# A delta-rule attention and a maxout network in one kernel: the third group's triangle moves from PSUM to SBUF, and the opening is reordered

## Chip, cores and metric

One NeuronCore of a Trainium2 chip. The metric is device time in microseconds (us), the median of several runs; lower is better.

## What is computed

Two layers. The first is a delta-rule recurrence over 768 positions for 4 batches x 8 heads with head size 48; its output, turned into 3072 rows of 384, goes through a feed-forward layer that takes the maximum of three products.

```python
k_n = k / (np.linalg.norm(k, axis=-1, keepdims=True) + 1e-06)
for t in range(S):
    y[:, :, t] = einsum('bhd,bhde->bhe', q[:, :, t], state)
    v_old = einsum('bhde,bhd->bhe', state, k_n[:, :, t])
    state = state + beta_t * einsum('bhd,bhe->bhde', k_n[:, :, t], v[:, :, t] - v_old)
x = y.transpose(0, 2, 1, 3).reshape(B * S, H * D)
h = maximum(maximum(x @ w1, x @ w2), x @ w3)
out = h @ w_out
```

## The kernel before

**Chunks, units, groups.** The sequence is cut into 12 chunks of 64 positions. A chunk is two *units* (half the batches each), so there are 24 units; two chunks make a *group* (6 in all), and one group gives 512 rows (a *piece*) of the feed-forward layer. Within a chunk the recurrence becomes linear algebra: the products of keys with keys (tile `at`) and of keys with queries (tile `pt`), and a triangular system whose inverse (`ut`) is applied to the values.

**From keys to the inverse.** `turn` transposes keys (part 0) or queries (part 1) of a unit on TensorE (PE) into PSUM and copies them to `kqt`; `gram` (`keys` for part 0 alone) makes the products `p_g` and copies them to `at` or `pt`. `to_blocks` and `first_blocks` bring the first group's 32 x 32 diagonal blocks into `x_bl` by copies and a transpose on VectorE (DVE); later groups go through DRAM (`to_dram`, `blocks`). `solve(m)` inverts a group's blocks by a chain of small DVE operations (L570, L574), one pair for each row. It starts with the norms of the keys (`norm`, from the diagonal of the block). The triangle is built in `y_bl` in SBUF, but for groups 1 and 2 in a PSUM tile `y_p`, which ScalarE (ACT) clears first and from which two copies (L576, L578) bring it back. The first group is solved only in blocks of 16 (`FINE`); `halves_t`, `halves_z`, `halves_u` join these to 32, and `turn_t1`, `join_z`, `join_u` join 32 to 64. Results go back to `ut` with a minus sign, by `negated`.

**Links.** Per chunk: `old_k` (values minus keys times state), `old_q` (queries times state), `new` (`p_u`, the updates `u`), `step` (adds to the state `st`), `to_y` (`p_y`), `to_x` or `y_blocks`/`read_y`/`turn_y` (the output turned into `xt`). The values are multiplied by the norms with `scale` on GpSimd (POOL, L287). For the first two chunks the norms come from squares and row sums of the keys themselves (`first_squares`, `flipped`, `first_norms`).

**Feed-forward.** `ffn(m)` yields after each product `p_h` (L935); the first three column blocks of piece 0 are made in halves of 256 rows (18 products), all others with 512. Then come the output products `p_o` (L967). The result of `p_h` is copied by ACT (L943) or joined by a maximum on DVE (L949).

**Weights.** They lie in 64 bits. `fetch` brings a piece to `w_bits` (5 buffers); each step of the generator `weights` has ACT make three conversions of one piece (L238 to L240, into `mant` and `up`, two buffers each), and then, for the piece before it, a DVE shift (L250) and a POOL addition (L254).

**PSUM.** All results of small products share the tag "two" (three buffers of two banks); `p_h`, `p_o` and `p_m` share the tag "ffn" (two buffers).

**Order.** It is written by hand: each engine executes its instructions in the order in which the program issues them. The opening (L1003 to L1088) is a plain list. Then the loop over `ffn(0)` (L1149) issues after each yield what the tables `FIRST` (links of chunk 1, queries), `EARLY_LINKS` (group 1), `CONVERTED` (steps that convert a weight piece) and `FETCHED` name; later pieces use `LINKS`. A letter in a table is a function (`z` join_z, `j` join_u, `k` old_k, `q` old_q, `u` new, `s` step, `y` to_y, `x` to_x, `e` halves_z, `f` halves_u, `d` turn_t1, `S` steps of the solver, `T` turn, `P` gram), the digit its chunk or unit.

Of the kernel before, what the change touches and what calls it, by code (L numbers as in the profile page):

```python
# [18 lines left out]
BL = 32  # L19
# [4 lines left out]
def kernel(  # L24
# [274 lines left out]

    ksum_0, kflip_0 = small("ksum0", 2, 2, H), small("kflip0", 2, H)  # L300

    def first_squares(units=range(4)):
        ksum, kflip, squares = ksum_0, kflip_0, []
        for n in units:
            c, g = divmod(n, 2)
            if n < 2:
                ksq = work.tile([128, H, D], FP32, name="ksq", tag="o_sb")
            else:
                ksq = in_wo(1).rearrange("p s r -> p (s r)")[
                    :, (n - 2) * H * D : (n - 1) * H * D  # L310
                ].rearrange("p (h d) -> p h d", h=H)
            nc.scalar.square(ksq, kpad[n][:, :, 0:D])
            squares.append(ksq)
        yield
        for n in units:
            c, g = divmod(n, 2)
            ksq = squares[n]
            nc.vector.tensor_reduce(
                out=kflip[:, c] if g else ksum[:, c, 0], in_=ksq,
                axis=mybir.AxisListType.X, op=ALU.add,  # L320
            )

    def flipped(kflip):
        p_n = ps_ffn([128, TOK], "p_n")[:, 0 : 2 * H]
        for bb in range(2):
            half = rows(1 - bb)
            nc.tensor.matmul(
                p_n[rows(bb)], ident[half, half],
                kflip[half].rearrange("p c h -> p (c h)"),
            )  # L330
        return p_n

    def first_norms():
        norm(nrm_0, ksum_0, small("root0", 2, 2, H), small("newton0", 2, 2, H))
# [186 lines left out]
    def solve(m):  # L521
# [8 lines left out]
        if m in (1, 2):  # L530
            y = ps_two("y_p").rearrange("p b (j i) -> p (b j) i", i=BL)
        if m:
            zero = kpad[0][:, 0:1, D : D + 1]
            nc.scalar.copy(y, zero.to_broadcast(y.shape))
        else:
            nc.gpsimd.memset(y_bl, 0.0)
# [4 lines left out]
        nc.vector.reciprocal(bl, bl)  # L541
        nc.vector.tensor_tensor(out=bl, in0=bl, in1=bl, op=ALU.mult)
        nc.vector.tensor_tensor(out=bl, in0=bl, in1=beta_bl[:, m] if m else beta_0, op=ALU.mult)
        if m > 2:
            nc.scalar.copy(diagonal(y), bl)
        else:
            (nc.vector if m else nc.gpsimd).tensor_copy(diagonal(y), bl)
# [10 lines left out]
        for j in range(size - 1):  # L558
# [16 lines left out]
            if m in (1, 2) and j == BL - 8:  # L575
                nc.scalar.copy(done[:, :, 0:HB], y[:, :, 0:HB])  # L576
            elif m in (1, 2) and j == BL - 2:
                nc.vector.tensor_copy(done[:, :, HB:BL], y[:, :, HB:BL])  # L578
            yield
        if m == 0:  # L580
# [3 lines left out]
            for cc in range(2):  # L584
                for i in range(4):
# [6 lines left out]
                    if half:  # L592
                        nc.scalar.copy(to, of)
                    else:
# [75 lines left out]

    def span(hs):
# [16 lines left out]
    def negated(bb, to, of, c=0):  # L688
        if bb and c < 1:
            nc.vector.tensor_scalar_mul(to, of, -1.0)  # L690
        else:
            nc.scalar.mul(to, of, -1.0)

    def halves_u(c):
        t, z = fine.pop(c), zs[c % NU]
        for hs, p_v, _ in heads_of(c, "p_f", BL):
            for i, h in enumerate(hs):
                for bb, g in TILES:
                    r = rows(bb ^ g)
                    nc.tensor.matmul(p_v[rows(bb), g, i], t[g][r, h], z[r, g, h])  # L700
            for f in (0, 1):
                for bb in range(2):
                    r = block(bb, f, HB)
                    negated(
                        bb,
                        ut[c % NU][r, :, span(hs), BL * f + HB : BL * (f + 1)],
                        p_v[r, :, :, HB * f : HB * (f + 1)],
                        c,
                    )

    def join_z(c):
        at = [ats.pop(2 * c + g) for g in range(2)]
        z, second = zs[c % NU], ut[c % NU][:, :, :, BL:C]
        for hs, p_v, _ in heads_of(c, "p_z", BL):
# [6 lines left out]
            nc.scalar.copy(z[block(0), :, span(hs)], p_v[block(0)])  # L721
            copy = nc.vector.tensor_copy if c < 1 else nc.scalar.copy
            copy(z[block(1), :, span(hs)], p_v[block(1)])

    def join_u(c):
        z, t = zs[c % NU], t1[c % NU]
        u12 = ut[c % NU][:, :, :, BL:C]
        for hs, p_v, _ in heads_of(c, "p_j", BL):
            for i, h in enumerate(hs):
                for bb, g in TILES:  # L730
                    r = block(bb ^ g)
                    nc.tensor.matmul(p_v[block(bb), g, i], t[r, g, h], z[r, g, h])  # L732
            for bb in range(2):
                negated(bb, u12[block(bb), :, span(hs)], p_v[block(bb)], c)
# [505 lines left out]
```

## Time and profile before

| | us |
|---|---|
| median of 3 runs | 524.41 |
| those runs | 521.0 to 526.13 |
| profiled execution, own time | 523.37 |
| its span on the core | 521.7 |
| PE busy in the span | 494.0 (95%) |
| DVE busy | 302.0 (58%) |
| POOL busy | 186.2 (36%) |
| ACT busy | 167.0 (32%) |

The profile shows one execution. Times in it count from the start of its span, so the 1.67 us between span and execution lie around it. Its views: the span in 40 slices of 13 us, with the busy tenths of each engine and the clock granted to PE; the busy time of each engine by stage; the timeline of one engine (start, length, operation, and in brackets the idle time before it with what ended it); the list of waits. "PEld" is PE's loading of the stationary operand, "issue" is time in which the engine waited for nothing that the profile shows.

### The profile page before, as it was taken

To read this page: it belongs to the slowest core of one execution; us is meant where nothing else is said; L and a number is where in the kernel's file an instruction comes from. 1 tells how busy PE (TensorE), PEld (TensorE's weight loads), DVE (VectorE), ACT (ScalarE), POOL (GpSimd) and SP (SyncE) were. 2 spreads that over 40 slices of the span, in tenths; PEclk is the share of its full clock that TensorE was granted. 3 is DMA by queue.
4 is the path that set the end of the run, shared out by engine and by line. 5 is a ranking of instruction groups with operands and counts; after the bars stand their busy time and mean duration, and the time that the engine had idled before them with its cause. 6 is when DMAs were issued, how large, how long until landed. Compare 5 with 4: busy or idle time off the path is not lost.

```text
span 521.7 us, 18025 instructions
## 1 busy us (share of the span) xinstructions
PE 494.0 (95%) x7840; PEld 305.5 (59%) x7840; DVE 302.0 (58%) x699; ACT 167.0 (32%) x306; POOL 186.2 (36%) x310
## 2 busy tenths in 40 slices
PE   7667799999899999999999999999999999999996
PEld 6556678845566555665555565655655555654453
DVE  5866998788695441699562988645896221111100
ACT  5557565875413142200143101252101411011000
POOL 6515073772292844851385770503130000000000
PEclk9756999999899999999999999999999999999999
DMA  8973968773035954454585553923334202220011
GB/s 116 215 153 100 172 170 132 184 213 90 3 91 135 183 94 100 104 127 113 116 154 116 127 133 88 171 43 92 81 97 96 41 3 63 61 61 0 0 30 31
DMA packets 108670, 53.45 MB, mean 102 GB/s; under 512 B 91760, under 2 KB 102928, under 8 KB 108592
## 3 DMA queue, kind: packets, MB, share of 16 engines
q1 hardware_dynamic: 97840, 34.44, 32.4%
q0 software_dynamic: 8640, 17.49, 14.0%
q8 instruction: 61, 1.00, 0.9%
q10 hardware_dynamic: 2112, 0.39, 0.5%
q14 instruction: 17, 0.14, 0.1%
HBM read 39.17 MB, written 13.11 MB: 100 GB/s over the span
## 4 chain that ended last, share of the span: by engine, by line
PE 81%; DVE 10%; ACT 3%; POOL 2%; issue 1%; DMA 1%; SPq 0%; DVEq 0%; POOLq 0%; ACTq 0%
PE p_h L935 36%; PE p_o L967 26%; PE p_g L438 4%; PE p_u L777 2%; PE p_m L915 2%; PE p_y L819 2%; PE p_s L800 2%; PE p_q L749 2%; PE p_k L749 2%; PE p_j L732 1%; DVE tmp L570 1%; PE p_z L718 1%; POOL w_sb L254 1%; PE p_t L361 1%; DMA kpad<-in_k_dram 1%
## 5 line engine op out<-in xcount | busy, mean ns | idle before, releaser
L935 PE MATMUL p_h<-xt,w_sb 128*128 128x512 f32 (+1 forms) x522 | 217.7, 561 | 1.7 <-DVE xt L886 1.3
L935 PEld LDWEIGHTS p_h<-xt,w_sb 128*128 128x128 f32 x522 | 95.2, 191 | 86.9 <-issue 80.3
L967 PE MATMUL p_o<-wo_sb,h 128*128 128x384 f32 x288 | 97.8, 489 | 0.0
L949 DVE TENSOR_TENSOR h<-h,p_h 128x512 f32<-128x512 f32 (+1 forms) x48 | 29.6, 617 | 93.9 <-PE p_h L935 93.8
L967 PEld LDWEIGHTS p_o<-wo_sb,h 128*128 128x128 f32 x288 | 53.8, 190 | 35.6 <-issue 0.5
L973 ACT COPY o_sb<-p_o 128x384 f32<-128x384 f32 x24 | 11.5, 479 | 131.3 <-PE p_o L967 128.2
L945 ACT ACTIVATE h<-p_h 128x512 f32<-128x512 f32 x30 | 17.9, 597 | 87.7 <-PE p_h L935 84.7
L967 PE MATMUL p_o<-w_sb,xt 128*128 128x384 f32 x120 | 42.0, 486 | 0.0
L570 DVE TENSOR_TENSOR tmp<-x_bl,y_bl 128x60 f32<-128x60 f32 (+19 forms) x108 | 38.8, 360 | 3.3
L396 POOL DMA_DIRECT2D turned<-in_q_dram x72 | 39.1, 551 | 4.4 <-POOL turned L391 2.6
L574 DVE TENSOR_TENSOR y_bl<-y_bl,tmp 128x60 f32<-128x60 f32 (+19 forms) x108 | 35.7, 330 | 3.7
L438 PE MATMUL p_g<-kqt 48*64 48x64 f32 (+1 forms) x1216 | 28.1, 243 | 7.0 <-DVE nt_bl L263 3.8
L438 PEld LDWEIGHTS p_g<-kqt 48*64 48x64 f32 x1216 | 25.0, 143 | 15.4 <-ACT kqt L367 8.1
L967 PEld LDWEIGHTS p_o<-w_sb,xt 128*128 128x128 f32 x120 | 22.8, 190 | 15.9
L254 POOL TENSOR_TENSOR w_sb<-mant,up 128x384 int32<-128x384 int32 x18 | 18.5, 1027 | 27.4 <-DVE mant L250 26.6
L120 POOL DMA_DIRECT2D kpad<-in_k_dram x32 | 21.8, 689 | 16.4 <-PE p_s L800 14.9
L287 POOL TENSOR_TENSOR v_t<-v_t,nrm 128x768 f32<-128x768 f32 x12 | 17.7, 1482 | 25.7 <-DVE nrm L266 14.2
L807 DVE TENSOR_TENSOR st<-st,p_s 48x768 f32<-48x768 f32 (+1 forms) x18 | 17.1, 950 | 15.3 <-PE p_s L800 15.1
L422 DVE TENSOR_TENSOR pt<-p_g,mask 128x512 f32<-128x512 f32 x20 | 13.8, 690 | 17.4 <-PE p_g L438 17.4
L574 DVE TENSOR_TENSOR y_p<-y_p,tmp 128x31 f32<-128x31 f32 (+15 forms) x62 | 21.6, 349 | 2.1
L139 POOL DMA_DIRECT2D v_t<-in_v_dram x12 | 9.9, 828 | 35.3 <-PE p_u L777 35.3
L391 POOL MEMSET turned<- 128x96 f32 x18 | 3.3, 191 | 46.6 <-DVE kqt L412 46.6
(158 smaller groups left out, 631.8 us busy)
## 6 DMA issues: line engine op xcount, KB each, us to landing
w_bits<-in_moe_w_dram SPq DMA_DIRECT2D x14, 384.0 KB, 5.5
out_dram<-o_sb SPq DMA_DIRECT2D x48, 96.0 KB, 2.2
turned<-in_q_dram POOLq DMA_DIRECT2D x72, 48.0 KB, 2.8
kpad<-in_k_dram POOLq DMA_DIRECT2D x32, 96.0 KB, 5.2
y_x<-y SPq DMA_DIRECT2D x16, 192.0 KB
qall<-y_x SPq DMA_DIRECT2D x32, 96.0 KB, 2.7
ut<-y_d SPq DMA_DIRECT2D x40, 64.0 KB, 2.8
v_t<-in_v_dram SPq DMA_DIRECT2D x12, 192.0 KB, 6.2
```

The costliest lines, as they stand in the source:

```text
L120: queues[bb].dma_start(out=dst[rows(bb ^ g), :, 0:D], in_=src[2 * bb + g, :, c * C : (c + 1) * C, :].rearrange("h p d -> p h d"),)
L254: nc.gpsimd.tensor_tensor(out=dst.bitcast(I32), in0=mant_v.bitcast(I32), in1=up_v, op=ALU.add)
L287: nc.gpsimd.tensor_tensor(out=vts[c], in0=vts[c], in1=nrm[:, :, :, None].to_broadcast([128, 2, H, D]), op=ALU.mult,)
L396: (queue, nc.gpsimd)[i].dma_start(out=t[p0 : p0 + 32, bb, at : at + NP * 2 * D].rearrange("p (j x) -> p j x", j=NP), in_=(k, q)[i][2 * bb ...
L438: nc.tensor.matmul(p_g[rows(bb ^ (g * i)), par, c0 : c0 + C * (1 + whole)], kq[:, 0], kq if whole else kq[:, i],)
L570: nc.vector.tensor_tensor(out=t_v, in0=row.to_broadcast(t_v.shape), in1=column.to_broadcast(t_v.shape), op=ALU.mult,)
L574: nc.vector.tensor_tensor(out=rest, in0=rest, in1=t_v, op=ALU.subtract)
L749: nc.tensor.matmul(p_b[rows(bb), par, c0 : c0 + D], kqt[g][dims(par), j, bb ^ g, i], st[dims(par), bb ^ g, g, j],)
L935: nc.tensor.matmul(p_h, w_sb[i][:, t, f * 128 : (f + 1) * 128], xt[:, t, lo : lo + w], start=(t == 0), stop=(t == KT - 1),)
L945: nc.scalar.activation(out=h, in_=p_h, func=mybir.ActivationFunctionType.Relu)
L949: nc.vector.tensor_tensor(out=h, in0=h, in1=p_h, op=ALU.max)
L967: nc.tensor.matmul(p_o, stays, moves, start=(n == 0), stop=(n == len(terms) - 1))
```

## The change

- **Third group.** `solve(2)` builds its triangle in `y_bl` in SBUF, as the first group does: POOL clears it and copies the diagonal into it. Only group 1 stays in PSUM.
- **Norms of the first two chunks.** Squares, row sums and the exchange through PE go. `solve(0)` keeps the norms in `bl` and puts the inverse into a tile of its own (`inv_bl`); `first_norms` is one DVE transpose of `bl`.
- **Opening.** Other engines copy `at`, the blocks and the solved blocks. The transposes and products of the queries of units 0 to 3 are all issued ahead of `halves_z(0)`. The solved blocks of chunk 1 and its `scale` are issued after `new(0)` and the third conversion. `halves_z(1)` leaves the opening for step 0 of piece 0 (`e1`), and the links of chunk 1 in `FIRST` move one step back.
- **First chunk's links.** `negated_of` gives the first half of the heads one PSUM tile that ACT alone negates, and the second half two tiles, one for ACT and one for DVE. `join_z` copies with ACT alone. `to_x(0)` uses one PSUM tile for each half.
- **Conversions.** One more weight piece is converted in the opening and one fewer in piece 0 (step 1 goes); at step 18 the conversion is issued behind the links instead of ahead of them.

```diff
--- before.py
+++ after.py
@@ -296,42 +296,10 @@
 
 
     nrm_0 = const.tile([128, 2, 2, H], FP32, name="nrm_0")
-
-    ksum_0, kflip_0 = small("ksum0", 2, 2, H), small("kflip0", 2, H)
-
...
+    bl_0 = []
 
     def first_norms():
-        norm(nrm_0, ksum_0, small("root0", 2, 2, H), small("newton0", 2, 2, H))
+        nc.vector.transpose(out=nrm_0.rearrange("p c g h -> p (c g h)"), in_=bl_0[0])
 
 
     kqts, ats, pts, xs, at_d = {}, {}, {}, {}, {}
@@ -527,24 +495,28 @@
         else:
             y_bl = work.tile([128, 2, HB * BL + HB], FP32, name="y_bl", bufs=1)
         done = y = in_rows(y_bl)
-        if m in (1, 2):
+        if m == 1:
             y = ps_two("y_p").rearrange("p b (j i) -> p (b j) i", i=BL)
-        if m:
+        if m in (0, 2):
+            nc.gpsimd.memset(y_bl, 0.0)
+        else:
             zero = kpad[0][:, 0:1, D : D + 1]
             nc.scalar.copy(y, zero.to_broadcast(y.shape))
-        else:
-            nc.gpsimd.memset(y_bl, 0.0)
         bl = small("bl", BL)
         norm(bl, diagonal(x), small("root_bl", BL), small("nt_bl", BL))
         if m:
             norms_of(m, bl)
-        nc.vector.reciprocal(bl, bl)
+            nc.vector.reciprocal(bl, bl)
+        else:
+            bl_0.append(bl)
+            bl = small("inv_bl", BL)
+            nc.vector.reciprocal(bl, bl_0[0])
         nc.vector.tensor_tensor(out=bl, in0=bl, in1=bl, op=ALU.mult)
         nc.vector.tensor_tensor(out=bl, in0=bl, in1=beta_bl[:, m] if m else beta_0, op=ALU.mult)
         if m > 2:
             nc.scalar.copy(diagonal(y), bl)
         else:
-            (nc.vector if m else nc.gpsimd).tensor_copy(diagonal(y), bl)
+            (nc.vector if m == 1 else nc.gpsimd).tensor_copy(diagonal(y), bl)
         if m < FINE:
             size, xv, yv = HB, in_blocks(xs[m]), in_blocks(y_bl)
             xb = xv[:, :, :, 0:HB]
@@ -572,9 +544,9 @@
                 in1=column.to_broadcast(t_v.shape), op=ALU.mult,
             )
             nc.vector.tensor_tensor(out=rest, in0=rest, in1=t_v, op=ALU.subtract)
-            if m in (1, 2) and j == BL - 8:
+            if m == 1 and j == BL - 8:
                 nc.scalar.copy(done[:, :, 0:HB], y[:, :, 0:HB])
-            elif m in (1, 2) and j == BL - 2:
+            elif m == 1 and j == BL - 2:
                 nc.vector.tensor_copy(done[:, :, HB:BL], y[:, :, HB:BL])
             yield
         if m == 0:
@@ -589,8 +561,11 @@
                         "p g h i -> p (g h) i"
                     )
                     of = back[r, :, 16 * cc : 16 * (cc + 1)].rearrange("p i x -> p x i")
-                    if half:
+                    if i == 1:
                         nc.scalar.copy(to, of)
+                    elif i == 3 and not cc:
+                        nc.vector.tensor_copy(to[:, 0:H], of[:, 0:H])
+                        nc.scalar.copy(to[:, H : 2 * H], of[:, H : 2 * H])
                     else:
                         (nc.gpsimd if cc else nc.vector).tensor_copy(to, of)
                 yield
@@ -668,6 +643,18 @@
                 p_v.rearrange("p g (h x) -> p g h x", x=w), copy,
             )
 
+    def negated_of(c, name, w):
+        if c:
+            p_v = ps_two(name)[:, :, 0 : H * w].rearrange("p g (h x) -> p g h x", x=w)
+            yield range(H), (p_v, p_v), (nc.scalar.mul,) * 2
+            return
+        p = [
+            ps_two(name)[:, :, 0 : NP * w].rearrange("p g (h x) -> p g h x", x=w)
+            for _ in range(3)
+        ]
+        yield range(NP), (p[0], p[0]), (nc.scalar.mul,) * 2
+        yield range(NP, H), (p[1], p[2]), (nc.scalar.mul, nc.vector.tensor_scalar_mul)
+
     def span(hs):
         return slice(hs[0], hs[-1] + 1)
 
@@ -685,27 +672,20 @@
                     )
             copy(zs[c % NU][:, :, span(hs)], p_v)
 
-    def negated(bb, to, of, c=0):
-        if bb and c < 1:
-            nc.vector.tensor_scalar_mul(to, of, -1.0)
-        else:
-            nc.scalar.mul(to, of, -1.0)
-
     def halves_u(c):
         t, z = fine.pop(c), zs[c % NU]
-        for hs, p_v, _ in heads_of(c, "p_f", BL):
+        for hs, p_v, negate in negated_of(c, "p_f", BL):
             for i, h in enumerate(hs):
                 for bb, g in TILES:
                     r = rows(bb ^ g)
-                    nc.tensor.matmul(p_v[rows(bb), g, i], t[g][r, h], z[r, g, h])
+                    nc.tensor.matmul(p_v[bb][rows(bb), g, i], t[g][r, h], z[r, g, h])
             for f in (0, 1):
                 for bb in range(2):
                     r = block(bb, f, HB)
-                    negated(
-                        bb,
+                    negate[bb](
                         ut[c % NU][r, :, span(hs), BL * f + HB : BL * (f + 1)],
-                        p_v[r, :, :, HB * f : HB * (f + 1)],
-                        c,
+                        p_v[bb][r, :, :, HB * f : HB * (f + 1)],
+                        -1.0,
                     )
 
     def join_z(c):
@@ -718,20 +698,19 @@
                     nc.tensor.matmul(
                         p_v[block(bb ^ g), g, i], at[g][r, h, 0:BL], second[r, g, h]
                     )
-            nc.scalar.copy(z[block(0), :, span(hs)], p_v[block(0)])
-            copy = nc.vector.tensor_copy if c < 1 else nc.scalar.copy
-            copy(z[block(1), :, span(hs)], p_v[block(1)])
+            for bb in range(2):
+                nc.scalar.copy(z[block(bb), :, span(hs)], p_v[block(bb)])
 
     def join_u(c):
         z, t = zs[c % NU], t1[c % NU]
         u12 = ut[c % NU][:, :, :, BL:C]
-        for hs, p_v, _ in heads_of(c, "p_j", BL):
+        for hs, p_v, negate in negated_of(c, "p_j", BL):
             for i, h in enumerate(hs):
                 for bb, g in TILES:
                     r = block(bb ^ g)
-                    nc.tensor.matmul(p_v[block(bb), g, i], t[r, g, h], z[r, g, h])
+                    nc.tensor.matmul(p_v[bb][block(bb), g, i], t[r, g, h], z[r, g, h])
             for bb in range(2):
-                negated(bb, u12[block(bb), :, span(hs)], p_v[block(bb)], c)
+                negate[bb](u12[block(bb), :, span(hs)], p_v[bb][block(bb)], -1.0)
 
 
     xts, rhss, qss, us, yts = {}, {}, {}, {}, {}
@@ -827,18 +806,24 @@
         if m not in xts:
             xts[m] = work.tile([128, KT, TOK], FP32, name="xt")
         y_f = yts.pop(c).rearrange("p g h d -> p g (h d)")
+        xt = xts[m][:, :, cc * 256 : (cc + 1) * 256].rearrange(
+            "p t (g x) -> p g t x", g=2
+        )
         p_x = ps_two("p_x")
         for g in range(2):
+            if g and not c:
+                p_x = ps_two("p_x")
             for t in range(KT):
                 nc.tensor.transpose(
                     p_x[:, g, t * 128 : (t + 1) * 128],
                     y_f[:, g, t::KT],
                     ident,
                 )
...
-        copied(c, xt, p_x[:, :, 0 : KT * 128].rearrange("p g (t x) -> p g t x", t=KT))
+            of = p_x[:, :, 0 : KT * 128].rearrange("p g (t x) -> p g t x", t=KT)
+            if not c:
+                (nc.vector.tensor_copy if g else nc.scalar.copy)(xt[:, g], of[:, g])
+        if c:
+            nc.scalar.copy(xt, of)
 
     yds, yqs = {}, {}
 
@@ -876,15 +861,6 @@
             ),
             in_=yqs.pop(c).rearrange("p b (x t) -> p b t x", t=KT),
         )
-
...
     def less_first(f):
         part = (slice(None), slice(None), slice(f * 128, (f + 1) * 128))
@@ -1013,26 +989,22 @@
     busy(6, ident)
     turn(0, (0,))
     turn(1, (0,), nc.vector.tensor_copy)
-    sums_0 = first_squares()
-    some(sums_0, 1)
-    keys(0, None, nc.vector.tensor_copy)
-    some(sums_0, 1)
-    keys(1, None)
-    to_blocks(0, (nc.gpsimd,) * 4)
+    A, V, P = nc.scalar, nc.vector, nc.gpsimd
+    keys(0, None)
+    to_blocks(0, (P, P, P, P))
     turn(2, (0,))
+    keys(1, None, nc.vector.tensor_copy)
+    to_blocks(1, (V, V, V, P))
     turn(3, (0,))
-    to_blocks(1, (nc.gpsimd,) * 4)
-    keys(2, None, nc.vector.tensor_copy)
+    keys(2, None)
+    to_blocks(2, (A, P, A, P))
     keys(3, None, nc.vector.tensor_copy)
-    to_blocks(2, (nc.scalar, nc.gpsimd, nc.scalar, nc.gpsimd))
-    to_blocks(3, (nc.vector, nc.scalar, nc.vector, nc.scalar))
+    to_blocks(3, (V, A, V, P))
     first_blocks()
     load_q(2, (nc.gpsimd, nc.gpsimd))
-    some(solving, 1)
-    p_n = flipped(kflip_0)
-    nc.scalar.copy(ksum_0[:, :, 1], p_n.rearrange("p (c h) -> p c h", c=2))
     turn(4, (0,))
     turn(5, (0,))
+    some(solving, 1)
     keys(4)
     keys(5)
     turn(6, (0,))
@@ -1040,26 +1012,26 @@
     load_q(3, (nc.gpsimd, nc.gpsimd))
     load_beta()
     keys(6)
+    turn(7, (0,))
     gram(0, (1,), None, later=True)
-    turn(7, (0,))
     keys(7)
-    turn(1, (1,))
-    gram(1, (1,), None, later=True)
     for _ in range(2):
         fetch(nc.sync)
     blocks(1)
     load_v(1)
+    turn(1, (1,))
+    some(conv, 1)
     turn(2, (1,))
+    gram(1, (1,), None, later=True)
+    turn(3, (1,))
     gram(2, (1,), None, later=True)
-    turn(3, (1,))
+    gram(3, (1,), None, later=True)
     some(solving, HB + 1)
     halves_t(0)
     halves_z(0)
-    gram(3, (1,), None, later=True)
     first_norms()
-    for c in range(2):
-        scale(c, nrm_0[:, c])
     some(conv, 1)
+    scale(0, nrm_0[:, 0])
     halves_u(0)
     turn_t1(0)
     join_z(0)
@@ -1068,18 +1040,18 @@
     masked(pts[1], by_par(pts[1]))
     old_k(0)
     old_q(0)
-    some(solving, 1)
     new(0)
     some(conv, 1)
     fetch(nc.sync)
+    some(solving, 1)
+    scale(1, nrm_0[:, 1])
     to_y(0)
     some(conv, 1)
     fetch(nc.sync)
-    halves_z(1)
     to_x(0)
+    halves_t(1)
     some(conv, 1)
     fetch(nc.sync)
-    halves_t(1)
     for n in (2, 3):
         masked(pts[n], by_par(pts[n]))
     load_q(4)
@@ -1103,8 +1075,8 @@
 
 
     FIRST = {
-        0: "f1 s0 S1 S1", 1: "z1 d1 S1 k1 S1 S1", 2: "j1 S1 S1 S1",
-        3: "S1 q1 S1 S1", 4: "u1 T4", 5: "y1", 6: "s1 T5", 7: "x1 T6",
+        0: "e1 s0 S1 S1", 1: "f1 k1 S1 S1 S1", 2: "z1 d1 S1 S1 S1",
+        3: "j1 S1 q1 S1 S1", 4: "u1 T4", 5: "y1", 6: "s1 T5", 7: "x1 T6",
         8: "T7", 14: "P4", 15: "P5", 21: "P6", 22: "P7",
     }
 
@@ -1144,14 +1116,14 @@
 
 
 
-    CONVERTED = {*range(6), *range(11, 25)}
+    CONVERTED = {0, *range(2, 6), *range(11, 25)}
     FETCHED = {8: 1, 12: 1, 13: 1, 14: 1, 18: 2, 19: 2, 20: 1, 21: 1}
     for i, _ in enumerate(ffn(0)):
         if 0 < i < 7:
             fetch(nc.sync)
         for _ in range(FETCHED.get(i, 0)):
             fetch(nc.gpsimd)
-        if i in (18, 25):
+        if i == 25:
             some(conv, 1)
         if i == 20:
             solving = solve(2)
@@ -1160,7 +1132,7 @@
             some(solving, 3)
         queries(FIRST.get(i, ""))
         links(1, EARLY_LINKS.get(i, ""))
-        if i in CONVERTED and i != 18:
+        if i in CONVERTED:
             some(conv, 1)
         if 3 < i < 14:
             some(solving, (2, 1, 2, 2, 3, 3, 3, 3, 2, 2)[i - 4])
```

## The prediction

> **What bounds the kernel now.** Line numbers are those of the kernel before. I read the page's slices first, then the busy time by stage, then what TensorE (PE) waited for, then the timelines of each engine where it waited.
>
> ```profile
> PE   7667799999899999999999999999999999999996
> ...
> PEclk9756999999899999999999999999999999999999
> ```
> ```profile
> 0.00:72.00 72.00, 52.27 (x1390) 43.82 (x1390) 55.36 (x140) 44.31 (x89) 31.23 (x56) 0.81 0.80 154
> 72.00:140.00 68.00, 64.56 (x1387) 46.19 (x1388) 56.65 (x132) 43.39 (x81) 35.19 (x43) 0.97 0.58 134
> 140.00:390.00 250.00, 249.86 (x3928) 146.99 (x3927) 162.64 (x377) 59.53 (x105) 119.77 (x212) 1.00 0.52 112
> ```
>
> The second fence has, after the stretch, its length and the busy us of PE, PE's weight loads, DVE, ACT and POOL, then the granted clock. From 140 us on PE is full (249.86 of 250) at clock 1.00, and its list of waits for that part is empty: there the kernel is PE-bound, and a change pays only by letting PE begin that dense part sooner. Only the two first stages have something to give: 19.7 us idle at clock 0.81, then 3.4 us idle at 0.97. In the second, two waits concern the change:
>
> ```profile
> 125.63 0.70 PE L438 MATMUL p_g<-kqt 48*64 48x64 f32 x32 [0.70 <-DVE pt L422]
> ...
> 133.76 4.29 PE L935 MATMUL p_h<-xt,w_sb 128*128 128x512 f32 x6
> ```
> ```profile
> 132.49 0.33 PE L749 MATMUL p_q<-st,xt 48*64 48x48 f32 x8 [1.38 <-DVE v_t L761]
> ```
>
> Columns: start, length, what, and in brackets the idle time ahead and its releaser. p_g needs nothing of pt, p_q nothing of v_t: each waits for its buffer. Of three "two" buffers in PSUM the third group's triangle (y_p) holds one, so p_q reuses p_k's, which DVE frees at 132.4 only. The product after that takes 4.29 us where its neighbours take 2.84: the clock is at 0.50 from 133.3 to 136.7.
>
> **The change, part by part, against the profiled span of 521.7 us.**
>
> *Third group in SBUF.* Removed: ACT's clearing of y_p (1.03), the two copies back (ACT 0.58, DVE 0.69) and the hold on a PSUM buffer. Added: a POOL memset (0.98, the row of the first group's) and the diagonal on POOL (0.69, likewise) in place of DVE's 0.20. That copy is hidden under the 1.22 us multiply L556, POOL being idle from 114.5 to 123.7; uncovered it would cost 0.5. The steps cost the same: their median is 328 and 342 ns in SBUF, 355 and 366 in PSUM. With three buffers p_g takes p_u's, freed at 121.0, and p_q takes that p_g's, freed at 127.9: both waits go, 0.70 + 1.38. What is late next is p_u at 138.0, which needs v_t itself (132.4): it has room.
>
> Here a rule speaks on the size. The Trainium skill ("TensorE: Matmul & The Clock Gate", Part 1) has the clock fall to half after about 3.4 us of idleness. By that, gaps this short cost no clock, and the sum is 2.1. The trace shows the fall at 133.3 after a stretch of 3.4 us in which PE was busy for 2.0. I take the trace: without the gaps the product is back at 2.84 (1.45), p_q saves 0.2, the sum is 3.7.
>
> A rule against the change: the same skill ("SBUF — State Buffer", Who interferes with whom) says that a DVE instruction with two SBUF inputs and a GpSimd one that reads SBUF exclude each other. In PSUM each step had one SBUF input; now it has two. The trace agrees in part:
>
> ```profile
> 41.29 1.72 DVE L422 TENSOR_TENSOR pt<-pt,mask 128x512 f32<-128x512 f32 x1
> ...
> 43.82 0.69 DVE L422 TENSOR_TENSOR pt<-pt,mask 128x512 f32<-128x512 f32 x1
> ```
> ```profile
> 40.98 1.47 POOL L287 TENSOR_TENSOR v_t<-v_t,nrm 128x768 f32<-128x768 f32 x1 [2.53 <-DMA v_t<-in_v_dram]
> 42.40 3.04 POOL L595 COPY ut<-x_bl 32x512 f32<-32x512 f32 x2
> ```
>
> The same mask took 1.72 beside POOL's multiply and 0.69 beside its copies. Between 123 and 131 POOL has three 1.0 us additions (L254). By the rule they hold DVE up to 3.0 us, half of that on average; by the undisturbed row nothing. v_t has 2.0 us before p_u wants it, so I take 0 and keep 1.0 as the bad end.
>
> *Conversion at step 18 behind the link.* z of the second group no longer waits behind a conversion (p_j waited 0.94 + 0.36 at 112). But p_s at 121.0 follows ACT's u copy (120.15), which follows the root at 118.66, and that waits for the loaded x_bl; this load follows stores issued by POOL in the old order. What p_j gains, p_s waits: I take 0, at best 1.3.
>
> *Opening.* I replay the new order with the old durations.
> Squares (4 x 0.5 ACT), sums (4 x 0.5 DVE) and p_n go; block copies are spread so that the transpose L503 starts at about 12.4 instead of 13.16: 0.7. The solve itself (to 29.13) is unchanged: 28.4.
> Copies to ut: DVE 0.6 + 0.6 + 0.35, ACT 1.05 + 0.55, side by side, ready at 30.0 instead of 31.89 (ACT came late, behind a query copy until 29.73, and had 2.1): 1.9. The queries' transposes and products are done by about 27, in PE's idle time.
> p_e 2.0, then DVE's transposes, p_f 32.25 to 34.25 (before 34.5 to 36.4; 1.1 us of query products stood between). The negations were eight in turn on ACT and DVE from 36.94, behind a conversion; now four on ACT run under the second half, two each after it: ready at 35.0 instead of 39.09.
> p_z and p_j end at 37.8 instead of 42.04; the last negation is no longer behind the 1.72 us mask: 38.4 instead of 43.79. u at 40.6 instead of 46.06. y and its transposes: piece 0's first product at about 45 instead of 50.69. So far 5.7 us.
>
> The gain does not stay. POOL's order is: first addition, v_t of chunk 0, second addition, *three* ut copies of chunk 1 (it was two), v_t of chunk 1, third addition. The second addition waits for DVE's shift, queued behind the u copy: POOL starts it at 40.95. Then 1.0 + 3 x 1.49 + 1.47 + 1.0 gives 49.0 for the third. ACT's fifth conversion reuses that addition's buffer, and behind it on ACT stand the clearing of y_p, the root, the h copy and chunk 1's z:
>
> ```profile
> 48.26 1.00 POOL L254 TENSOR_TENSOR w_sb<-mant,up 128x384 int32<-128x384 int32 x1 [0.76 <-DVE mant L250]
> 50.96 1.00 POOL L254 TENSOR_TENSOR w_sb<-mant,up 128x384 int32<-128x384 int32 x1 [1.70 <-DVE mant L250]
> ```
> ```profile
> 52.24 0.25 ACT L261 ACTIVATE root_bl<-wo_sb 128x32 f32<-128x32 f32 x1
> ```
>
> So 49.0 + 1.4 + 1.0 + 0.25: the root ends at 51.7 instead of 52.5. DVE then has the second group's set-up and the state (54.15 to 59.36 before, 5.2 us): 56.9. p_k starts at 57.0 instead of 59.42, a gain of 2.4. Up to p_y (72.05) the queues keep that: one more piece is converted ahead, so u no longer waits behind POOL's four key loads (66.0 to 68.7), and p_j waits 1.1 for DVE's transposes instead.
>
> But PE now has done its work ahead of p_k and stands idle from about 54 to 57. By the skill's 3.4 us the clock would hold and 2.4 remain. By the row at 133 it falls; 3.4 us at half rate lose 1.7, of which 1.1 go into p_j's wait: 0.6. I take 1.8. The ends: -1.5 (POOL's copies or the clock cost three more), +3.5 (the links, now nearly gapless from 30 to 42, reach full clock).
>
> Sum: 1.8 + 3.7 = 5.5. Span 516.2; the profiled execution's 523.37 becomes 517.9; the median of the runs shown, 524.41, is 1.0 above that execution and becomes 518.9.
>
> **Rivals.**
> *The gain passes in full:* opening 3.5, p_j's 1.3 and 3.7: 8.5, 515.9. For it: the dense links. Against it: x_bl's load and POOL's queue, both in order.
> *The opening gives nothing:* POOL's queue and the idle gap eat all of it, the third group remains: 524.4 - 3.7 = 520.7. For it: the root moves by 0.8 only.
> *The third group's waits come back* as DVE waits behind POOL's additions, and the clock falls all the same: 524.4 - 1.8 = 522.6. For it: the 1.72 us row. Against it: the steps are short, and 2.0 us of room.
> *Slower:* three copies on POOL are held by DVE's own SBUF work; each us that the third addition ends after 51.5 delays p_k by one beyond today's. From 55.2 the whole is slower than before; at 60.5, twelve late, it gives 529.7. It needs each of POOL's six instructions to wait two us. The rows of such copies, 1486 to 1499 ns beside a busy DVE, speak against it.
> The buffer's release is sure, so a change that does nothing is no separate case.
>
> **How the numbers follow.** A measurement of this kernel tells about 1% (5.2 us) from no change. Likeliest 0.46, 518.9, own range 517.0 to 521.0, two thirds of it under 519.2; gain in full 0.16; no gain in the opening 0.24, an eighth of it below 519.2; waits come back 0.08; slower 0.06. Faster by over 1%: 0.31 + 0.16 + 0.03 = 0.50; slower by over 1%: 0.05; within: 0.45. The range takes in the full gain and the waits' return, with half a us around each: 515 to 523.
>
> **What would show it.** Right: y_p gone after 120 us, no waits before p_g and p_q, the following product at 2.84 and clock 1.00 near 133; L503 at 12.4; piece 0's first product near 45; three ut copies on POOL from 42 to 46.5, root at 51.5, p_k near 57; p_s waiting for u. Wrong: root later than 52.5 or before 50; steps of the third group above 0.5 us beside L254; new PE waits after 140.

## Result and profile after

| | before | after |
|---|---|---|
| median | 523.88 us (20 runs) | 519.43 us (20 runs, 516.98 to 526.79) |
| profiled execution, its span | 523.37, 521.7 | 520.86, 519.2 |

The ratio is 0.9911, 95% interval [0.9884, 0.9937]: 4.7 us faster. It leaves out the one run after (526.79) that was in a slower state, while the medians in the table include it. A second measurement, beside the experiments, gave 0.9923 [0.9897, 0.9949]. The forecast of 518.9 was 0.5 us off, and that close partly by luck: it took 5.5 us off 524.41, the median of three runs, where 20 runs of the kernel before give 523.88. Its two terms are another matter; below they are taken apart. Line numbers are now those of the changed kernel.

The slices of the page after, with PE's busy tenths and granted clock, and the stages with the columns as before:

```profile
PE   7767799999999999999999999999999999999996
...
PEclk9756799999999999999999999999999999999999
```
```profile
0.00:72.00 72.00, 54.05 (x1384) 45.13 (x1385) 52.77 (x130) 42.17 (x87) 30.82 (x54) 0.76 0.80 153
72.00:140.00 68.00, 66.58 (x1436) 47.05 (x1436) 56.24 (x128) 43.41 (x81) 37.14 (x45) 1.00 0.58 135
```

The second stage is nearly full now, at clock 1.00: of its 1.4 idle us 1.07 stand ahead of p_s. The first is not full: PE still idles 18 us of 72, at a lower clock than before (0.76, was 0.81).

*Third group.* PE's timeline of after, where p_g and p_q waited before:

```profile
125.77 0.69 PE L406 MATMUL p_g<-kqt 48*64 48x64 f32 x32
...
131.06 0.30 PE L728 MATMUL p_q<-st,xt 48*64 48x48 f32 x8
...
132.11 2.84 PE L911 MATMUL p_h<-xt,w_sb 128*128 128x512 f32 x6
134.88 1.15 PE L756 MATMUL p_u<-v_t,ut 64*64 64x48 f32 x64
```

No bracket stands behind p_g and p_q any more, and the product that took 4.29 takes 2.84. From p_s (121.91) to the product after p_u and p_x (136.75) 14.84 us pass; before it was 18.81 (121.04 to 139.85). The price is there too: DVE's steps beside POOL's additions, from the two engines' timelines.

```profile
129.93 1.06 DVE L546 TENSOR_TENSOR y_bl<-y_bl,tmp 128x112 f32<-128x112 f32 x1
131.02 0.30 DVE L542 TENSOR_TENSOR tmp<-x_bl,y_bl 128x135 f32<-128x135 f32 x1
...
133.81 0.95 DVE L740 TENSOR_TENSOR v_t<-v_t,p_k 128x768 f32<-128x768 f32 x1
```
```profile
129.84 1.01 POOL L254 TENSOR_TENSOR wo_sb<-mant,up 128x384 int32<-128x384 int32 x1 [0.46 <-DVE mant L250]
```

The step beside the addition takes 1.06, the larger one behind it 0.30. A second such step at 124.79 took 0.90. Together that is some 1.4 us ahead of v_t, which ends at 134.76; p_u starts at 134.88. The room is just used up, so what the steps lost beside POOL cost nothing here.

*Opening.* The first product of piece 0 starts at 47.67 (before 50.69), but p_k, the state's first use, gains 0.6 only (58.80 against 59.42). POOL, ACT and PE of after:

```profile
44.93 3.33 POOL L570 COPY ut<-x_bl 32x512 f32<-32x512 f32 x3
48.34 1.47 POOL L287 TENSOR_TENSOR v_t<-v_t,nrm 128x768 f32<-128x768 f32 x1
49.77 1.00 POOL L254 TENSOR_TENSOR w_sb<-mant,up 128x384 int32<-128x384 int32 x1
```
```profile
50.81 0.57 ACT L238 ACTIVATE mant<-w_bits 128x384 f32<-128x384 f32 x1 [3.19 <-POOL w_sb L254]
...
53.25 0.25 ACT L261 ACTIVATE root_bl<-wo_sb 128x32 f32<-128x32 f32 x1
```
```profile
58.80 1.96 PE L728 MATMUL p_k<-st,kqt 48*64 48x48 f32 x64 [3.38 <-DVE st L786]
60.69 2.93 PE L911 MATMUL p_h<-xt,w_sb 128*128 128x256 f32 x6
```

The three copies stand ahead of the third addition, ACT waits 3.19 us for that, PE idles 3.38 ahead of p_k, and after the gap the granted clock is 0.50 until 64.5 (p_k took 1.15 before, p_h 1.56). Chunk 1's p_y starts at 72.64, 0.6 later than before. So in this execution, whose span is 2.5 us shorter than before, the whole gain lies behind the opening, in the stretch of the third group.

### The profile page after: what moved, and what is told of

It is laid out like the page before. It is cut to its first block, busy times and chain, and to the rows that moved or that the text cites. A ratio compares the mean times of both kernels' runs of the same rounds, so it can differ in the third digit from the quotient of the medians.

```text
span 519.2 us, 18006 instructions
## 1 busy us (share of the span) xinstructions
PE 495.1 (95%) x7836; PEld 306.1 (59%) x7836; DVE 301.3 (58%) x687; ACT 163.4 (31%) x302; POOL 188.3 (36%) x311
## 4 chain that ended last, share of the span: by engine, by line
PE 83%; DMA 5%; DVE 3%; ACT 3%; SPq 2%; POOL 2%; issue 1%; ACTq 0%; POOLq 0%
PE p_h L911 36%; PE p_o L943 26%; PE p_g L406 4%; PE p_u L756 3%; PE p_k L728 2%; PE p_m L891 2%; PE p_y L798 2%; PE p_q L728 2%; SPq L120 2%; PE p_s L779 2%; PE p_j L711 2%; DMA w_bits<-in_moe_w_dram 1%; DMA x_bl<-at_d 1%; PE p_z L698 1%; PE p_t L329 1%
## 5 line engine op out<-in xcount | busy, mean ns | idle before, releaser
L546 DVE TENSOR_TENSOR y_bl<-y_bl,tmp 128x31 f32<-128x31 f32 (+20 forms) x139 | 50.5, 363 | 4.8
L542 DVE TENSOR_TENSOR tmp<-x_bl,y_bl 128x31 f32<-128x31 f32 (+20 forms) x139 | 50.0, 360 | 4.1
L406 PEld LDWEIGHTS p_g<-kqt 48*64 48x64 f32 x1216 | 24.7, 142 | 12.4 <-issue 6.2
L702 ACT COPY z<-p_z 32x512 f32<-32x512 f32 (+1 forms) x26 | 14.1, 542 | 17.5 <-PE p_z L698 17.0
```

The costliest lines, as they stand in the source:

```text
L406: nc.tensor.matmul(p_g[rows(bb ^ (g * i)), par, c0 : c0 + C * (1 + whole)], kq[:, 0], kq if whole else kq[:, i],)
L542: nc.vector.tensor_tensor(out=t_v, in0=row.to_broadcast(t_v.shape), in1=column.to_broadcast(t_v.shape), op=ALU.mult,)
L546: nc.vector.tensor_tensor(out=rest, in0=rest, in1=t_v, op=ALU.subtract)
```

## Experiments

All ratios are to the kernel before, measured beside it on the same chip. "Changed kernel" is the kernel after.

**The two parts alone.** Third group only: the kernel before with this edit.

```diff
-        if m in (1, 2):
+        if m == 1:
             y = ps_two("y_p").rearrange("p b (j i) -> p (b j) i", i=BL)
-        if m:
+        if m in (0, 2):
+            nc.gpsimd.memset(y_bl, 0.0)
+        else:
             zero = kpad[0][:, 0:1, D : D + 1]
             nc.scalar.copy(y, zero.to_broadcast(y.shape))
-        else:
-            nc.gpsimd.memset(y_bl, 0.0)
...
-            (nc.vector if m else nc.gpsimd).tensor_copy(diagonal(y), bl)
+            (nc.vector if m == 1 else nc.gpsimd).tensor_copy(diagonal(y), bl)
...
-            if m in (1, 2) and j == BL - 8:
+            if m == 1 and j == BL - 8:
...
-            elif m in (1, 2) and j == BL - 2:
+            elif m == 1 and j == BL - 2:
```

> The kernel before with one edit: the third group's triangle is built in SBUF. My theory: nearly all of the change's gain is here: -3.7 to -4.0 us, ratio 0.993; no waits before p_g and p_q near 125 and 132, the product after them at 2.84 us with the clock at 1.00. Rival, the gain comes from the opening: 0 to -1 us here, ratio 0.998 to 1.000.

Measured: 521.44 us, 0.9963 [0.9946, 0.998], that is -1.9 us. The trace shows what was expected (14.86 us from p_s to the product, p_q without a wait), yet the time gains half of it. One trace is a weak witness here: up to chunk 1's p_y this program is the kernel before, and yet this execution comes to it 2.6 us later than the trace of before (74.66 against 72.05).

Opening only: the changed kernel with that edit undone.

> The changed kernel with the third group's triangle back in PSUM; the rebuilt opening and the conversion at step 18 stay. My theory: the opening gives little, -0.5 to -1.8 us, ratio 0.9965 to 0.999; p_y of chunk 1 within 1 us of its old place, the waits before p_g and p_q back. Rival, the opening brings the gain: -4 us or more, ratio 0.992 or lower.

Measured: 522.07 us, 0.9988 [0.9962, 1.0013], -0.6 us, which can't be told from nothing. PE in its trace, same place, triangle in PSUM:

```profile
130.70 0.33 PE L728 MATMUL p_q<-st,xt 48*64 48x48 f32 x8 [0.56 <-DVE v_t L740]
...
131.78 2.84 PE L911 MATMUL p_h<-xt,w_sb 128*128 128x512 f32 x6
```

Here p_q waits 0.56 only, p_g not at all, and the clock stays: the product behind takes 2.84, not 4.29. From p_s to the product after p_u and p_x 15.57 us pass, 0.7 more than with the triangle in SBUF, where the trace of before had 4.0 more. It is tempting to read this as two prices of one wait, with the clock lost and without. But PE had lost its time already, 24 us earlier:

```profile
106.70 0.25 PE L698 MATMUL p_z<-ut,at 32*32 32x32 f32 x4 [0.91 <-ACT h L919]
...
108.08 4.34 PE L911 MATMUL p_h<-xt,w_sb 128*128 128x512 f32 x6
```

So PE is late against the other engines in this execution: the root of the third group's set-up starts 4.1 us ahead of p_s here, and 2.3 to 2.4 in the traces of before, third group only and the changed kernel. So DVE freed the buffer sooner, and 0.56 is not the price of the same wait. A longer stretch, from chunk 1's p_y to the product after p_u and p_x, takes both places in: 67.80 us before, 64.27 third group only, 64.11 and 63.85 in two traces of the changed kernel, and 66.38 here. By single traces the hold thus costs 3.5 without the new opening, and at most 2.3 to 2.5 with it (the waits before p_z come ahead of the third group's triangle, and nothing shows that they belong to the hold).

The Trainium skill ("TensorE: Matmul & The Clock Gate", Part 1) says that the window of about 3.4 us over which the clock is decided runs freely, so that the moment of a change depends on where in it the matmuls fall. The forecast cited the 3.4 us and passed over this. By it, the same hold could cost the clock in one execution and not in another; no run here shows that it does.

The four times put together (523.5 before; -1.9 and -0.6 alone; -4.7 and -4.0 together): the third group brings 1.9 without the opening and some 3.7 with it, mean 2.8; the opening 0.6 and some 2.4, mean 1.5. Each time has an uncertainty of 0.9 to 1.4 us, and a difference of two up to 1.9, so this doesn't show that the parts help each other. Nor do the traces explain why the third group alone gains 1.9 and not 3.5.

**Conversion at step 18 ahead of the links again**, in the changed kernel.

```diff
-        if i == 25:
+        if i in (18, 25):
             some(conv, 1)
...
-        if i in CONVERTED:
+        if i in CONVERTED and i != 18:
             some(conv, 1)
```

> The changed kernel with the conversion of step 18 again ahead of the links. My theory, what p_j gains p_s waits: p_j near 112 waits 1.0 to 1.3 again, the wait before p_s near 121 (1.1) shrinks by the same, the time within 0.5 us of the changed kernel. Rival, the move brings its 1.3 us: 1.0 to 1.5 us slower than the changed kernel.

Measured: 519.16 us, 0.9913 [0.9882, 0.9944]; the changed kernel beside it 519.62, 0.9923. PE's waits from 72 to 140 us, with this edit and then without:

```profile
PE p_z L698 <- ACT up L240: 0.7, 1, 0.7
PE p_j L711 <- ACT z L702: 0.4, 1, 0.4
```
```profile
PE p_s L779 <- ACT u L761: 1.1, 1, 1.1
```

1.1 us before p_z and p_j, or 1.1 us before p_s (0.8 in the second trace of the changed kernel): the wait moves and about keeps its size.

**Copies early**: chunk 1's ut copies and scaling leave their place behind new(0).

```diff
     old_q(0)
+    some(solving, 1)
+    scale(1, nrm_0[:, 1])
     new(0)
     some(conv, 1)
     fetch(nc.sync)
-    some(solving, 1)
-    scale(1, nrm_0[:, 1])
```

> The changed kernel with the copies of chunk 1's solved blocks and its scaling issued ahead of new(0), when POOL stands idle (37 to 44 us), instead of behind new(0) and a conversion. My theory, POOL's queue holds the third addition and so ACT's conversion, the root and p_k: third addition near 47 instead of 50.8, root near 50.3 instead of 53.4, p_k near 56 instead of 58.8, the clock does not fall to half, 2 to 3.6 us faster than the changed kernel (about 516, ratio to before 0.985 to 0.988). Rival, the opening is bound by something else (loads, the solver's DVE work): no more than 0.5 us.

Measured: 518.54 us, 0.9902 [0.9859, 0.9944], not told apart from the changed kernel. POOL was freed as expected (third addition 47.14, root 50.58), but p_k came at 58.86, no earlier. DVE of this kernel:

```profile
51.39 2.09 DVE L390 TENSOR_TENSOR pt<-pt,mask 128x512 f32<-128x512 f32 x2
53.41 0.17 DVE L262 TENSOR_SCALAR nt_bl<-root_bl 128x32 f32<-128x32 f32 x1
...
57.66 0.95 DVE L786 TENSOR_TENSOR st<-st,p_s 128x768 f32<-128x768 f32 x1
```

The set-up did not follow the root. DVE is busy with transposes and masks until 53.4 whatever the root does, then come 4.3 us of set-up, then the state. Two things hide a small gain, though. This execution was late before the edit could act: p_e of chunk 0 starts at 31.99 (30.89 in the changed kernel), the first product of piece 0 at 49.14 (47.67). And in the changed kernel POOL's copies held not only the root but also DVE's transposes:

```profile
48.30 0.71 DVE L630 STREAM_TRANSPOSE t<-ut 128x512 f32<-128x512 f32 x1 [1.00 <-POOL ut L570]
...
53.53 0.18 DVE L262 TENSOR_SCALAR nt_bl<-root_bl 128x32 f32<-128x32 f32 x1 [0.52 <-ACT root_bl L261]
```

Counted from the first product, p_k comes 9.7 us after it here, and 11.1 and 10.7 in the two traces of the changed kernel. So of the 2.7 us by which the root moves, 1.0 to 1.4 reach p_k, as far as single traces tell; DVE's own work takes the rest.

**Filler**: 14 unused products between p_f and p_k, to hold the clock (a new letter `B` in the table, which calls `busy(7 * n, ident)`).

```diff
-        0: "e1 s0 S1 S1", 1: "f1 k1 S1 S1 S1", 2: "z1 d1 S1 S1 S1",
+        0: "e1 s0 S1 S1", 1: "f1 B2 k1 S1 S1 S1", 2: "z1 d1 S1 S1 S1",
```

> The changed kernel with 14 products of the identity with itself (not used by anything) issued to TensorE between p_f and p_k of chunk 1, where it stands idle for 3.4 us. My theory, the clock falls because of that gap: the clock stays at 1.00 from 58 to 65, p_k takes 1.15 us instead of 1.96 and the product after it 1.6 instead of 2.9, chunk 1's p_y 1 to 1.7 us earlier, in all -0.5 to -1.5 us against the changed kernel. Rival, the slow clock there has another cause: no change of the clock and of the time, or later by what the products take beyond the gap.

Measured: 521.23 us, 0.9963 [0.9943, 0.9984]: about 2 us slower than the changed kernel. Its trace nevertheless shows that the gap is what slows p_k:

```profile
56.46 3.39 PE L974 MATMUL p_w<-ident 128*128 128x128 f32 x28
59.88 1.15 PE L728 MATMUL p_k<-st,kqt 48*64 48x48 f32 x64
61.40 1.53 PE L911 MATMUL p_h<-xt,w_sb 128*128 128x256 f32 x6 [0.37 <-DVE h L925]
```

A likely reason for the slower time: the filler is paid in every execution, but the gap is 3.4 us in one trace of the changed kernel, 2.6 in the other, 0.3 in the opening-only one, where PE came late because it ran slow earlier. The traces show these gaps; that they make the 2 us is argued, not shown.

**State first**: p_s and the addition to the state go right behind to_x(0).

```diff
     to_x(0)
+    step(0)
     halves_t(1)
...
-        0: "e1 s0 S1 S1", 1: "f1 k1 S1 S1 S1", 2: "z1 d1 S1 S1 S1",
+        0: "e1 S1 S1", 1: "f1 k1 S1 S1 S1", 2: "z1 d1 S1 S1 S1",
```

> The changed kernel with the first chunk's step(0), its products p_s and the addition to the state, issued right behind to_x(0), ahead of chunk 1's transposes, of the masks and of the second group's set-up on DVE. Theory now (after the copies-early kernel): p_k of chunk 1 is set by DVE's order, since the addition to the state stands behind the masks and 4.4 us of set-up: the addition near 49 instead of 57.8, p_k right behind p_f near 55.5 instead of 58.8, no idle time of PE there, p_y of chunk 1 at 68 to 70 instead of 72.6, and 2.5 to 4.5 us less than the changed kernel (ratio to before 0.983 to 0.986). My older theory, POOL's queue and the root set it: the same, since the root no longer stands ahead. Rival, later links or the second group's solver take it back: within 1 us of the changed kernel.

Measured: 520.82 us, 0.9932 [0.9906, 0.9957]. No gain. Now another queue, ACT's, holds PE: p_f waits for ACT's z copy, which stands behind the conversion that waits for POOL's third addition (51.02).

```profile
55.51 1.57 PE L681 MATMUL p_f<-z,t 64*64 64x32 f32 x64 [2.49 <-ACT z L673]
56.85 1.96 PE L728 MATMUL p_k<-st,kqt 48*64 48x48 f32 x64
```

**Both**: copies early and state first.

> The changed kernel with both moves: chunk 1's ut copies and scaling ahead of new(0), and step(0) right behind to_x(0). Theory: two queues hold p_k of chunk 1, one behind the other: DVE's (the addition to the state behind masks and set-up) and, once that is gone, ACT's (z behind a conversion that waits for POOL's third addition). With both gone: third addition near 47, no wait of PE over 0.5 us between the first product and p_k, p_k 7.5 to 8 us after the first product (11.1 in the changed kernel), p_y of chunk 1 at 68 to 70, and 2 to 3.5 us less than the changed kernel (ratio to before 0.985 to 0.988). Rival, TensorE's clock or later links take it back: within 1 us of the changed kernel.

Measured: 520.59 us, 0.9943 [0.9921, 0.9964]. p_k comes at 54.75 without a wait, as expected, 4 us earlier than in the changed kernel. After one more product and p_z, PE waits for DVE's maximum, queued behind the set-up, and loses the clock again:

```profile
60.74 2.90 PE L911 MATMUL p_h<-xt,w_sb 128*128 128x256 f32 x6 [2.69 <-DVE h L925]
```

**Four moves**: also the masks of units 2 and 3 in DVE's idle time before u, and chunk 1's values loaded ahead of the blocks.

```diff
-    blocks(1)
     load_v(1)
+    blocks(1)
...
-    masked(pts[1], by_par(pts[1]))
+    for n in (1, 2, 3):
+        masked(pts[n], by_par(pts[n]))
...
-    for n in (2, 3):
-        masked(pts[n], by_par(pts[n]))
```

> The kernel with both moves (chunk 1's ut copies and scaling ahead of new(0); step(0) right behind to_x(0)) and two more: the masks of units 2 and 3 go to DVE's idle time before u (40 to 42 us), and chunk 1's values are loaded ahead of the second group's blocks, so that POOL's scaling doesn't wait for them. Theory: with ACT and POOL free, PE's fourth product waits for DVE's maximum behind masks (2.1 us) and set-up (4.4): without the masks that wait falls from 2.7 to about 0.9, the clock isn't lost there, p_y of chunk 1 comes 20 to 21 us after the first product instead of 23 to 25, and the time is 3 to 4.5 us under the changed kernel: 515 to 516.5, ratio to before 0.983 to 0.986. Rival, each wait taken away in the opening gives its gain to the next, or to the clock: within 1.5 us of the changed kernel, 518 to 520.5.

Measured: 519.48 us, 0.9919 [0.9891, 0.9947]: the rival. The wait before that product fell to 1.1 as expected, and the next one came:

```profile
62.27 0.21 PE L711 MATMUL p_j<-z,t 32*32 32x32 f32 x2 [1.74 <-DVE t L616]
```

The opening of all these kernels side by side, from one trace each (us). The longest wait is PE's between the first product of piece 0 and chunk 1's p_y. In the last three kernels p_s stands ahead of the first product, which starts later for it.

| | first product | root | p_k | longest wait | p_y of chunk 1 | ratio |
|---|---|---|---|---|---|---|
| before | 50.7 | 52.2 | 59.4 | issue 1.4 | 72.1 | 1 |
| changed kernel | 47.7 | 53.3 | 58.8 | p_k 3.4 | 72.6 | 0.9911 |
| the same, second trace | 47.1 | 52.3 | 57.8 | p_k 2.6 | 70.4 | 0.9923 |
| filler | 48.8 | 54.3 | 59.9 | p_h 0.4 | 72.2 | 0.9963 |
| copies early | 49.1 | 50.6 | 58.9 | p_j 0.2 | 70.6 | 0.9902 |
| state first | 48.9 | 54.5 | 56.9 | p_f 2.5 | 71.2 | 0.9932 |
| both | 49.2 | 50.8 | 54.8 | p_h 2.7 | 72.4 | 0.9943 |
| four moves | 49.0 | 49.8 | 54.6 | p_j 1.7 | 70.9 | 0.9919 |

p_k moves by 5 us, p_y by 2, and but for the filler no time can be told apart from the changed kernel's.

**The stall in p_u.** PE stood still in the middle of p_u at 41 us with no semaphore to wait for. Three runs ask why. The second run of the changed kernel:

> The changed kernel itself, once more, beside the kernels of this call. Every theory: ratio to before 0.991, within 0.988 to 0.994. It gives a second trace of the same code: a stall of PE in the middle of p_u near 41 us that is a matter of the code would be there again, at the same product; a chance event would not.

The stall is at the same product (1.05 us this time, 1.82 the first). With a third of the bytes of five weight pieces:

```diff
+            few = 1 if 3 <= fetched[0] < 8 else a
             queue.dma_start(
-                out=st.rearrange("p (a b) -> p a b", a=a), in_=src
+                out=st.rearrange("p (a b) -> p a b", a=a)[:, 0:few],
+                in_=src[:, 0:few],
             )
...
-        for dst, _, (a, b) in pieces:
+        for at, (dst, _, (a, b)) in enumerate(pieces):
...
+            if 3 <= at < 8:
+                low, high = (t[:, 0:1].to_broadcast(t.shape) for t in (low, high))
```

> The changed kernel with a third of the bytes for weight pieces 4 to 8 (their first rows are used for all three parts of the piece, so the weights and the output are not the reference's): 1.28 MB less moved between 32 and 46 us, all instructions kept. Theory: PE's stall in p_u near 41 us (1.8 to 2.7 us, no semaphore) is code that arrives late because the loads fill the DMA engines: the stall falls below 0.5 us. Rival, a fixed price of that place in the code: it stays at 1.8 or more.

It is 0.92 us, which is what neither theory expected. With all loads in place the traces of this study have 0.63 to 2.66 us at this product, so one trace with 0.92 tells nothing on the loads. With the blocks' load moved behind the weights:

```diff
-    blocks(1)
     load_v(1)
...
     fetch(nc.sync)
+    blocks(1)
     for n in (2, 3):
```

> The changed kernel with the load of the second group's blocks (512 KB in packets of 128 bytes) behind the weight loads that wait for ACT, so that it starts near 44 us instead of 35. Theory: the stall in p_u is code of PE that arrives late behind these packets: stall below 0.5 us, first product of piece 0 about 1 us earlier, the time 0.5 to 1.5 us less than the changed kernel, unless the root now waits for the blocks. Rival, the stall doesn't depend on the loads: 1 to 2.7 us as before.

0.99 us, which tells as little, and 517.9 us, 0.9892 [0.9853, 0.993], again not told apart from the changed kernel. With eight more loads and matmuls ahead of p_e:

```diff
+    busy(4, ident)
     some(solving, HB + 1)
     halves_t(0)
```

> The changed kernel with 4 more products of the identity with itself (8 loads and 8 matmuls in the trace, used by nothing) ahead of p_e of chunk 0, where PE is idle. Theory: PE's stalls without a semaphore fall on the borders of blocks of 128 loads and 128 matmuls of code: the stall in p_u comes after 14 of its matmuls instead of 22. Rival, it belongs to the data or the buffers of p_u: after 22 as before.

PE in the changed kernel, and in this one:

```profile
38.86 0.89 PE L756 MATMUL p_u<-v_t,ut 64*64 64x48 f32 x22 [0.24 <-issue]
41.57 1.41 PE L756 MATMUL p_u<-v_t,ut 64*64 64x48 f32 x42 [1.82 <-issue]
```
```profile
38.68 0.67 PE L756 MATMUL p_u<-v_t,ut 64*64 64x48 f32 x14 [0.23 <-issue]
41.39 1.62 PE L756 MATMUL p_u<-v_t,ut 64*64 64x48 f32 x50 [2.04 <-issue]
```

Eight more ahead, and the stall comes eight matmuls earlier: it belongs to a place in PE's instruction stream, not to p_u. (Its one execution, 522.8 us, also had a wait of 1.6 us ahead of p_s near 122 us, and says nothing on what the 8 cost.)

## Why the forecast came out right, point by point

*Third group, 3.7: right in mechanism, too large where it stands alone.* Both waits went, in order and place; p_u got v_t in time, with 0.1 us left of 2.0. The times give 1.9 (1.0 to 2.8) alone and some 3.7 on top of the opening. The term that may be too large is the clock: 1.45 + 0.2 was taken in full from one execution. The opening-only trace has a shorter hold there and no loss of the clock, but also a different history, so it doesn't settle this.

*Contention on SBUF, 0 with 1.0 as the bad end: right, narrowly.* Single steps grew by 0.7 to 0.8 us beside POOL's additions. Two of them, 0.90 and 1.06 us long, passed the 0.5 that the forecast named as a sign of being wrong; the 1.4 us that they added ahead of v_t just fit into its room.

*Step 18, 0: right*, as far as undoing it shows: the traces have the same wait in another place, and the time is 0.5 us less, not 1.0 to 1.5 more, with some 1.5 us of uncertainty on each time.

*Opening, 1.8: right within its uncertainty (0.6 to 2.4), by other numbers, and so in part by luck.* The gain at p_k was forecast as 2.4 and is 0.6 and 1.6 in the two traces; chunk 1's p_y comes 0.6 later than before in one and 1.7 earlier in the other. The first product was forecast for 45 and came at 47.1 and 47.7, for three reasons that the replay did not hold. DVE's transpose started at 12.72, not 12.4. ACT, whose order now has a conversion among the query copies, waited until 24.98 for its weights, so ut was ready at 31.5, not 30.0, and p_e starts at 30.89, no earlier than before (30.86). And PE's stall in p_u: the replay had no row for it, since before it fell elsewhere (1.36 at 58.55).

*POOL's queue: right in order, too strong as the one cause.* The third addition ended at 50.8 and 49.8 (forecast 49.0): the second one had started at 44.0 and 43.0 instead of 40.95, and shorter copies made up for 1.1 us of it. The root ended at 53.5 and 52.5 (51.7; later than 52.5 was a sign of being wrong), p_k came at 58.8 and 57.8 (57.0). But freeing POOL moved the root by 2.7 us and p_k, counted from the first product, by 1.0 to 1.4. DVE's queue, from transposes through masks to the set-up, was nearly as late; the forecast had DVE wait for the root and left out the transposes and masks ahead of it.

*The idle gap drops the clock: right, under-sized.* Forecast 3 us of gap and a loss of 0.6; gaps of 3.4 and 2.6, and p_k, the product after it, p_z and the next product together took 2.9 us longer than at full clock in one trace (1.96, 2.93, 1.08, 1.94 against 1.15, 1.56, 0.75, 1.56), 1.6 in the other. The filler run, with p_k at 1.15, shows that the gap is the cause. p_j's wait of 1.1, which was to swallow most of it, did not come.

*Slower by POOL's copies:* they took 1.1 us each, not 1.49; in the changed kernel's two traces the third addition did not end after the 51.5 from which this rival counts.

What stays open: whether PE's stall in p_u depends on the loads that run beside it, why the filler kernel is slower by 2 us, why the third group alone gains half of what its trace shows, and the split of the gain more finely than one to two us. No run tries the new opening without the conversion among the query copies.

## What to carry to other kernels

Where four in-order queues end within a us or two of each other, an instruction that is late names one queue only; ask of each other queue when it would have been ready without it, for that difference is all that a repair can gain. A wait that can cost TensorE its clock has no single price: the gap ahead of p_k cost 2.9 us of slow work in one trace of the changed kernel and 1.6 in the other, so put the price with the fall and without it into the range. Before comparing a wait in two kernels, compare the stretch that leads up to it: a loss that has moved to an earlier place looks like a gain. Before reading a gain out of a pair of single traces, look at how far the same code moves between two of its own: here p_y of chunk 1 moved by 2.3 us.

## What the runs showed of the hardware

PE's stalls without a semaphore lie on a grid in its instruction stream. Counted in weight loads from the start they come after 723 in every trace of the changed kernel and of its variants, after 1105 and 1233 (before), 598 and 1105 (third group only), 597 (state first) and 1358 (both). Neighbours are 125 to 128 loads apart, and 723 and 1105 are 382, which is three times 128 less two. The page's line for the queue that carries code:

```profile
q8 instruction: 61, 1.00, 0.8%
```

61 packets make 1.00 MB, 16.4 KB each. The page counts 18,006 instructions, 1.14 MB with the 0.14 MB of a second such queue, so about 63 bytes each. By this estimate a packet holds about 256, that is 128 loads with their 128 matmuls. The Trainium skill ("Runtime: NRT & Kernel Launch", Instruction fetch mechanics) says the same of the block, 256 instructions, and calls crossing a border mostly hidden. Here most borders pass without a stall too, but every trace of this study has one or two where PE stood still for 0.5 to 2.7 us, all of them in runs of short matmuls (32 or 64 rows and columns). That it then waits for code is inferred from the grid and the packets; no view shows it.
